# Loading and normalizing the first token block in two column halves, one warm-up matmul fewer, and later logit sums, in a fused attention and gated-MLP kernel

## The chip, the cores and the metric

One NeuronCore of one Trainium2 chip. The metric is device time of one execution in microseconds (us); "span" is the shorter time that the profile shows between first and last instruction. In these kernels the time is the span plus 1.7 to 1.8 us.

Engine names in profile lines: PE is TensorE's matmuls, PEld its weight loads, DVE VectorE, ACT ScalarE, POOL GpSimd, SP SyncE. "SPq" is an instruction that the sync engine's sequencer spends on issuing a DMA.

## The reference

```python
xn = layernorm(x)                                  # x: 2048 tokens x 512, bf16
# A: 32 heads of 16, each query looks at 8 keys, 2 apart, behind it
qkv    = xn @ wqkv
logits = einsum('bhsd,bhswd->bhsw', q, gathered_k) * scale     # + mask
o      = einsum('bhsw,bhswd->bhsd', softmax(logits), gathered_v) @ wo
# B: MLP with a spatial gate
z  = gelu(xn @ w_in)                               # 2048 x 1792
z1 = z[:, :896];  z2 = layernorm(z[:, 896:])
g  = einsum('ts,bsf->btf', w_sp, z2) + b_sp        # w_sp: 2048 x 2048
return x + o + (z1 * g) @ w_out
```

## The kernel before

A planner gets tasks (`T(engine, function, reads, writes, est, name)`), orders them on each engine by estimates, and sets the semaphores. The order on an engine is fixed when the kernel is built; each engine then runs its tasks in that order. PE's tasks for this argument, in order: ten warm-up matmuls, the first block's transposes, the z2 stage (`z2`, with the right half of `w_in`), the projections Q and K, ..., the z1 stage, the logit sums scattered among these, then the spatial gate.

The loads at the start. x blocks are 128 tokens (128 KB). The z2 weights come in two column halves, "a" and "b", each split over the sync and the scalar queue:

```python
ld_x(0, "sp")                       # block 0, sync queue
ld_x(1, "act")                      # block 1, scalar queue
ld_win_h("w_in2a", FH, HF)          # first half of the z2 weights, on both queues
ld_x(2, "sp"); ld_x(3, "act")
ld_win_h("w_in2b", FH + HF, HF)     # second half, on both queues
...
```

The first block: statistics and aggregate on DVE, power on POOL, normalization on DVE, four transposes on PE, two evictions.

```python
def ln_block(b):
    T("dve", bn_stats(Fv("st6", 6, 9 * b), xin), reads=[("xin", xs_)] + ..., name="bnst%d" % b)
    T("dve", bn_aggr(...), name="bnag%d" % b)
    T("pool", tensor_tensor(rstd, mv, mhalf, ALU.pow), name="rstd%d" % b)
    T("dve", tensor_scalar(xn, xin, mean, rstd, subtract, mult), name="norm%d" % b)
    ...
    T("pe", tr, reads=[("xn", sl), "ident"], name="xTr%d" % b)      # four 128x128 transposes
    ...
```

The logit sums. VectorE multiplies queries by shifted keys into one of four product buffers `pb`; PE sums two buffers at a time with 16 matmuls. `margin` is how much later than a product's estimated end the planner puts its sum:

```python
T("dve", lambda v: v.tensor_tensor(pbv, qb, kb, ALU.mult), reads=rd, writes=[("pb", s_)], name="prod%d_%d" % (j, c), ...)
...
T("pe", mm, reads=[("pb", (s_ - 1) % NPB), ("pb", s_), "E8"], writes=["psl"],
  est=4 * 232.0 + 100, name="red%d_%d" % (j, c), margin=cfg.get("m_red", 800.0))
```

The last sum, `red3_3`, reads buffers 2 and 3. Behind it comes the spatial gate. It needs `w_sp` transposed, in four pieces of 2 MB (`wT0` to `wT3`) that take turns in two places. The second place lies on memory that the logit stage used:

```python
lay(base, ("Sn", 3 * NK * 384), ("wT1", WSL), ...)                # wT1: elements 9216 to 17408 from base
lay(base, ("QT", 4096), ("KT", 8 * (512 + KP)), ("pb", NPB * 4096))  # pb: buffer 2 begins at 16512
```

So `wT1` covers product buffers 0, 1 and the first 896 elements of buffer 2, and its load has to wait for the last logit sum. The first consumer of `wT1` on PE is a slice of four matmuls (`gp6_1_0`, line 1053 before, 1078 after), which stands between the fourth and the fifth of the seven products of the gate's first quarter. The products of each quarter also need differences within that quarter's `wT`, which VectorE makes: four instructions of 1.22 us per quarter, `T1`, `T2`, `T4` and `T3` with the quarter's number (line 960 before, 985 after). `T3_3`, of the last quarter, is the last of them.

## Time and profile before

| before | |
|---|---|
| time | 237.72 us, median of 3 (237.45 to 238.06) |
| span | 236.0 us |
| PE busy | 230.8 us (98%) |
| first z2 matmul / second weights' half used / first projection | 6.71 / 7.81 / 14.03 us |
| last logit sums / their wait for the product | 100.72 / 0.86 us |

The page's busy line, PE's waits, the first 7 us and the hole at 100 us are shown in the prediction. The timeline of PE around the gate's first products (start us, us, engine, line, operation, count): the products begin at 111.20 and run into the slice that uses `wT1` (line 1053) at 115.02. The first row hides a wait of 0.149 us for ScalarE, before the product at 113.26; the view breaks a row only from 0.15 us on.

```profile
111.20 3.98 PE L1098 MATMUL ps<-arena 128*128 128x256 bf16 x32
115.02 1.03 PE L1053 MATMUL ps<-arena 128*128 128x512 bf16 x4
```

```profile
199.47 2.35 DVE L960 TENSOR_TENSOR arena<-arena 128x2048 bf16<-128x2048 bf16 x2
```

```profile
201.99 1.25 PE L1098 MATMUL ps<-arena 128*128 128x256 bf16 x10
```

VectorE stands idle for 0.93 us for a power on POOL, starts again at 90.89, and in that trace has no idle time above 0.11 us until `T3_3` ends at 201.82 (199.47 plus 2.35). The product that needs it starts 0.17 us later. So PE and VectorE come to this meeting point at nearly the same time, and after it PE alone sets the 34.2 us to the end.

### The profile page before, as it was taken

The numbers are of one execution on the slowest core, as the hardware profiler recorded it, in microseconds if no ns is written. First come the engines' busy times: TensorE is split into PE (matmuls) and PEld (weight loads), VectorE is DVE, ScalarE is ACT, GpSimd is POOL, SyncE is SP. The second block draws the span as 40 slices with busy tenths as digits, with TensorE's granted clock in tenths as the row PEclk, the third lists the DMA queues.
The fourth block names the chain that finished last, engine by engine and source line by source line (L and its number), as shares of the span: only waits on it lengthen the run. The fifth ranks groups of instructions, "written<-read, shape, count | busy, mean of one in ns | idle before, by whom it ended". The sixth has DMA issues, their size and how long they took to land.

```text
span 236.0 us, 3886 instructions
## 1 busy us (share of the span) xinstructions
PE 230.8 (98%) x1511; PEld 138.0 (58%) x1511; DVE 203.4 (86%) x231; ACT 143.7 (61%) x303; POOL 44.1 (19%) x74
## 2 busy tenths in 40 slices
PE   7999999999999999999999999999999999999996
PEld 3444444444444444345787777776777677777753
DVE  4688789989989898999999999999999999998022
ACT  2698678958889996659543554453445444554512
POOL 4555846477054013000000000000000000000000
PEclk9999999999999999999999999999999999999999
DMA  6987999802009900059504697484993664122302
GB/s 202 355 215 204 258 316 304 115 0 78 13 0 209 238 0 0 0 128 269 185 0 93 236 288 209 159 238 110 280 332 88 224 131 183 44 60 56 87 25 89
DMA packets 61698, 35.53 MB, mean 151 GB/s; under 512 B 49388, under 2 KB 60012, under 8 KB 60656
## 3 DMA queue, kind: packets, MB, share of 16 engines
q1 hardware_dynamic: 55040, 27.96, 45.9%
q10 hardware_dynamic: 5824, 5.21, 6.9%
q0 software_dynamic: 816, 2.12, 3.5%
q8 instruction: 12, 0.20, 0.3%
q14 instruction: 6, 0.05, 0.1%
HBM read 19.01 MB, written 4.21 MB: 98 GB/s over the span
## 4 chain that ended last, share of the span: by engine, by line
PE 82%; issue 6%; ACT 5%; DVE 4%; POOLq 1%; POOL 1%; ACTq 0%
PE ps L1098 31%; PE ps L1200 16%; PE ps L733 11%; PE ps L861 8%; PE ps L1053 4%; PE ps L713 4%; PE ps L878 3%; PE ps L772 3%; PE ps L636 2%; DVE arena L759 2%; DVE arena L937 1%; POOLq L399 1%; ACT L809 1%; POOL vscr L720 1%; ACT arena L809 1%
## 5 line engine op out<-in xcount | busy, mean ns | idle before, releaser
L1098 PE MATMUL ps<-arena 128*128 128x256 bf16 x672 | 79.0, 273 | 0.2
L1098 PEld LDWEIGHTS ps<-arena 128*128 128x128 bf16 x672 | 65.5, 98 | 15.0 <-ACT ps L1026 0.7
L1026 ACT ACTIVATE arena<-ps 128x256 bf16<-128x256 f32 (+2 forms) x43 | 20.1, 468 | 39.9 <-PE ps L1098 21.2
L1200 PE MATMUL ps<-arena 128*128 128x512 bf16 (+2 forms) x187 | 41.9, 366 | 0.0
L1147 DVE TENSOR_TENSOR arena<-arena 128x4096 bf16<-128x4096 bf16 x16 | 36.6, 2290 | 0.8
L759 DVE TENSOR_TENSOR arena<-arena 128x4096 bf16<-128x4096 bf16 x16 | 36.1, 2284 | 0.0
L1156 DVE TENSOR_TENSOR arena<-arena 128x4096 bf16<-128x4096 bf16 (+2 forms) x24 | 33.6, 1399 | 0.9
L733 PE MATMUL ps<-arena 128*128 128x512 bf16 x128 | 28.8, 379 | 0.0
L1200 PEld LDWEIGHTS ps<-arena 128*128 128x128 bf16 x187 | 19.6, 108 | 13.8
L861 PE MATMUL ps<-arena 128*128 128x448 bf16 x128 | 26.1, 353 | 0.4 <-DVE arena L696 0.2
L878 PE MATMUL ps<-arena 128*128 128x512 bf16 x112 | 24.9, 379 | 0.2 <-ACT arena L883 0.2
L733 PEld LDWEIGHTS ps<-arena 128*128 128x128 bf16 x128 | 12.3, 98 | 15.5 <-issue 1.3
L741 ACT ACTIVATE arena<-ps 128x1024 bf16<-128x1024 f32 x16 | 16.3, 1019 | 7.0 <-PE ps L733 6.3
L1026 ACT ACTIVATE ps<-ps 128x256 f32<-128x256 f32 x36 | 13.2, 366 | 11.8 <-PE ps L1098 10.8
L960 DVE TENSOR_TENSOR arena<-arena 128x2048 bf16<-128x2048 bf16 x16 | 19.4, 1220 | 0.8 <-DMA arena<-in_B_w_sp_dram 0.4
L883 ACT ACTIVATE arena<-ps 128x512 bf16<-128x512 f32 x28 | 15.7, 605 | 6.7 <-PE ps L878 6.5
L866 ACT ACTIVATE arena<-ps 128x448 bf16<-128x448 f32 x32 | 17.2, 545 | 4.1 <-PE ps L861 1.9
L861 PEld LDWEIGHTS ps<-arena 128*128 128x128 bf16 x128 | 11.9, 98 | 13.2 <-ACT arena L866 1.3
L1026 ACT ACTIVATE ps<-arena 128x512 f32<-128x512 bf16 (+3 forms) x33 | 16.7, 509 | 4.5 <-ACT arena L1026 3.0
L878 PEld LDWEIGHTS ps<-arena 128*128 128x128 bf16 x112 | 10.7, 98 | 14.0 <-ACT arena L883 1.1
L1053 PE MATMUL ps<-arena 128*128 128x512 bf16 x64 | 15.6, 379 | 0.0
L888 ACT ACTIVATE arena<-arena 128x896 bf16<-128x896 bf16 x16 | 15.1, 946 | 0.2
(67 smaller groups left out, 217.3 us busy)
## 6 DMA issues: line engine op xcount, KB each, us to landing
arena<-vscr SPq DMA_DIRECT2D x8, 1152.0 KB, 6.0
arena<-in_A_x_dram ACTq DMA_DIRECT2D x18, 128.0 KB, 2.6
vscr<-arena POOLq DMA_DIRECT2D x16, 128.0 KB, 5.2
arena<-in_A_x_dram SPq DMA_DIRECT2D x14, 128.0 KB, 6.7
out_dram<-arena ACTq DMA_DIRECT2D x14, 128.0 KB, 1.8
arena<-in_A_wqkv_dram SPq DMA_DIRECT2D x2, 512.0 KB, 7.8
arena<-in_B_w_in_dram SPq DMA_DIRECT2D x1, 896.0 KB, 5.2
arena<-in_B_w_out_dram SPq DMA_DIRECT2D x1, 896.0 KB, 6.2
```

The source lines that it names most:

```text
L733: last = t.matmul(bank(k + which), AC(off["wqk"] + 1024 * dc + col0, [[1, 128]]), AC(off["xnT"] + dc * S + 512 * j, [[1, 512]]), start=(dc ...
L759: T("dve", lambda v: v.tensor_tensor(pbv, qb, kb, ALU.mult), reads=rd, writes=[("pb", s_)], est=c_dve(4096, 2.0), name="prod%d_%d" % (j, c ...
L861: last = t.matmul(ps[:, 512 * k: 512 * k + HF], AC(off["xnT"] + dc * S + 128 * b, [[1, 128]]), AC(off["w_in2"] + FH * dc + c0, [[1, HF]]), ...
L866: T("act", (lambda k, hf: lambda a: a.activation(A("z2", HF, FH * b + HF * hf), ps[:, 512 * k: 512 * k + HF], ACTF.Gelu_apprx_tanh, accum_ ...
L878: lastm = t.matmul(bank(k), AC(off["w_in1"] + FH * dc + 128 * fc, [[1, 128]]), AC(off["xnT"] + dc * S + 512 * j, [[1, 512]]), start=(dc == ...
L960: T("dve", (lambda o_, x_, y_: lambda v: v.tensor_tensor(o_, x_, y_, ALU.subtract))(o_, x_, y_), reads=rd, writes=[wr], est=c_dve(NK * 256 ...
L1026: T("act", lambda a: a.activation(out_, in_, ACTF.Copy), reads=reads, writes=writes, est=c_act(n), name=name)
L1053: last = t.matmul(bank(k), AC(off["z2"] + FH * sh + 128 * fc, [[1, 128]]), AC(WT[r_] + sh * 512, [[1, 512]]), start=False, stop=(sh == NB ...
L1098: last = t.matmul(half(bk), lh(k), rh(k), start=False, stop=(k == NK - 1), skip_group_check=True)
L1147: T("dve", (lambda tv, iv, av: lambda v: v.tensor_tensor(tv, iv, av, ALU.mult))(tv, iv, av), reads=[("attn", j)] + ([("Ve", par)] if q < 2 ...
L1156: T("dve", (lambda o_, n: lambda v: v.tensor_tensor(o_, two(0, n), two(n, n), ALU.add))(o_, n), reads=[] if n > 512 else ["Vs", ("Ve", par ...
L1200: last = t.matmul(po, lh, rh, start=False, stop=(q == len(order) - 1), skip_group_check=True)
```

## The change

Its intent: reach the first useful matmul sooner, by loading the first block as two column halves on two queues and letting the statistics, the normalization and the transposes work half by half; and close PE's hole before the last logit sums by letting the planner put them later. The core of the diff:

```diff
-    warm=10,
+    warm=9,
...
-        ld_x(0, "sp")
-        ld_x(1, "act")
+        for h in range(2):
+            dma(("sp", "act")[h], ... A("xin", 256, 256 * h), x2[0:128, 256 * h: 256 * h + 256] ...)
+        ld_x(1, "sp")
         ld_win_h("w_in2a", FH, HF)
...
+        def ln_first():
+            for h in range(2):
+                T("dve", bn_stats(st0[6 * h], xin half h), name="bnst0%s" % "ab"[h])
+            T("dve", bn_aggr(mv, Fv("st0", 15)), name="bnag0")
+            T("pool", ... pow ..., name="rstd0")
+            for h in range(2):
+                T("dve", tensor_scalar(xn half h, xin half h, ...), name="norm0%s" % "ab"[h])
+                T("pe", tr, ...two transposes..., name="xTr0%s" % "ab"[h])
+            ... the two evictions and the two fill matmuls as before
...
-                  est=4 * 232.0 + 100, name="red%d_%d" % (j, c), margin=cfg.get("m_red", 800.0))
+                  est=4 * 232.0 + 100, name="red%d_%d" % (j, c), margin=cfg.get("m_red", 1600.0))
```

Cut: the memory and the two memsets of the statistics (DVE has four instructions more), and the general path with its first-block cases taken out. One more load on the sync queue: block 1 moved there, so the weights' sync halves are each one issue later.

## The prediction

> **What bounds the kernel now.** I read the page's busy shares first, then who PE waited for, then the order of time in the first 14 us and around 85 to 116 us. The busy share says that PE is the engine to look at:
>
> ```profile
> PE 230.8 (98%) x1511; PEld 138.0 (58%) x1511; DVE 203.4 (86%) x231; ACT 143.7 (61%) x303; POOL 44.1 (19%) x74
> ```
>
> Those 98% also hold warm-up matmuls that compute nothing, and ends that are modelled, so I checked spacing. In the long runs 32 matmuls of 512 columns take 6.91 us (0.216 us each) and 16 of 256 columns take 1.75 us (0.109 us each). At that spacing PE runs nearly without a hole from 14 us to 231 us. So the time is: the start until PE's first useful matmul, plus PE's work, plus the few holes in it, plus a tail (last matmul ends near 233.7, span 236.0). The holes are short:
>
> ```profile
> PE ps L636 <- DVE fpool L545: 1.3, 1, 1.3
> PE ps L772 <- DVE arena L759: 0.9, 1, 0.9
> PE ps L861 <- DVE arena L696: 0.2, 1, 0.2
> PE ps L878 <- ACT arena L883: 0.2, 1, 0.2
> ```
>
> The columns are us in total, times, longest. The first is the wait for the zeros before the warm-up. The second is one wait of the logit sums (L772) for the last product (L759). The third is the end of the first block's preparation, the fourth a filled set of PSUM banks.
>
> The start, in order of time, from the chain's window and the timeline (start, us, what):
>
> ```profile
> 3.35 0.69 DVE L664 BATCH_NORM_STATS2 fpool<-arena 128x6 f32<-128x512 bf16 x1 [1.94 <-DMA arena<-in_A_x_dram]
> 4.07 0.20 DVE L667 BATCH_NORM_AGGREGATE fpool<-fpool 128x2 f32<-128x9 f32 x1
> 4.36 0.58 POOL L669 TENSOR_TENSOR fpool<-fpool 128x1 f32<-128x1 f32 x1 [1.59 <-DVE fpool L667]
> 4.97 0.41 DVE L671 TENSOR_SCALAR arena<-arena,fpool 128x512 bf16<-128x512 bf16 x1
> 5.44 0.42 PEld L686 LDWEIGHTS ps<-arena 128*128 128x128 bf16 x4 [0.64 <-DVE arena L671]
> 5.50 0.54 PE L686 MATMUL ps<-arena 128*128 128x128 bf16 x4
> 6.07 0.42 DVE L696 CAST arena<-ps 128x256 bf16<-128x256 f32 x1 [0.58 <-PE ps L686]
> 6.71 0.92 PE L861 MATMUL ps<-arena 128*128 128x448 bf16 x4 [0.25 <-DVE arena L696]
> ```
>
> It is one serial chain: load (issued at 0.80), statistics, aggregate, power on POOL, normalize, four transposes, two evictions in parallel, first z2 matmul at 6.71. The transposes' weights are loaded at 5.44, and their matmul starts at 5.50, when the tenth warm-up matmul ends (ten at 0.427 us from 1.26 give 5.5).
>
> The mid-kernel hole:
>
> ```profile
> 91.06 8.81 PE L878 MATMUL ps<-arena 128*128 128x512 bf16 x40
> 100.72 1.05 PE L772 MATMUL ps<-arena 128*32 128x512 bf16 x16 [0.86 <-DVE arena L759]
> 101.70 6.22 PE L878 MATMUL ps<-arena 128*128 128x512 bf16 x28
> ```
>
> PE does 40 z1 matmuls, then stands for the product, then does the logit sums, then 28 more z1 matmuls that could have gone first. VectorE ends that product at about 100.67 (96.18 plus 4.49).
>
> **What the Trainium skill says.** "TensorE: Matmul & The Clock Gate", What's actually happening: the array starts at half clock and is released after a busy window of about 3.4 us, whose phase is free-running. The trace agrees in kind: warm-up matmuls come 0.43 us apart, later ones 0.216. The same page's "Wait — 56ns, not 53.3ns?" gives 426.7 and 215.7 ns for 512 columns, as seen here. "DMA: Bandwidth & Descriptors", Issuing engines are not separate DMA queues: two issuers save issue time, not movement. The two first loads here, issued at 0.80 and 0.81 on two queues, indeed share the engines. "VectorE: DVE Perf Modes", TRN2 errata: each instruction pays a fixed extra, so halving the elements does not halve the time. This trace shows it: aggregation of 9 numbers takes 0.20 us and statistics of 512 take 0.69.
>
> **The change part by part.**
>
> 1. Load in halves. The first block's 128 KB is no longer one load beside the second block's 128 KB, but two of 64 KB, first on each queue; block 1 moves to second on the sync queue. So the engines move 128 KB instead of 256 KB before the first block is complete. At the page's 355 GB/s of the second slice the 128 KB less is 0.36 us at most; with 512-byte rows I take 0.25: statistics can start near 3.10 instead of 3.35.
> 2. Statistics in halves. 0.69 us for 512 elements, with about 0.16 us fixed (512 at 0.96 per ns would be 0.53; an estimate), gives 0.42 for 256; the second, back to back, saves 0.04 as the second 512-element one does (0.65). Together about 0.80 against 0.69: a loss of 0.11. Aggregate over 15 numbers: still 0.20.
> 3. Normalize in halves: 0.41 becomes about 0.27 twice, the second overlapped by some 0.03: 0.51, a loss of 0.10. But the first two transposes now lie beside the second half's normalization, and after it only two of four remain: two at 0.107 us cold, a gain of 0.21. Net gain 0.11.
> 4. One warm-up matmul fewer: PE is free at 5.07 instead of 5.50. By itself it gains the 0.06 us between the weights (5.44) and the matmul (5.50); otherwise it only removes a block that the earlier chain would now meet. Warm and ready by chain: norm ends near 5.3, last transposes near 5.6, evictions (0.42) end near 6.3, z2 starts near 6.5 instead of 6.71.
> Sum of the start: 0.25 - 0.11 + 0.11 + 0.06, about 0.3; I take 0.2, since the chain has semaphore hops that I can't halve.
>
> Does it survive to 14 us? The z2 stage is a relay between PE and ScalarE (gelu eviction, then the next block's transpose eviction, then PE again at 8.84 and 10.99), so an earlier first z2 moves the later ones. One absolute edge is the second half of the weights, used at 7.80 in the kernel before. Its sync half now has a block more ahead of it. I count half of the 0.2 as at risk there.
>
> 5. Logit sums later. The planner's margin before a sum goes from 800 to 1600 ns. PE's alternative work comes in z1 groups of four matmuls, 4 x 0.216 = 0.86 us, so 0.8 us more margin is about one group more in front of the sums. In the hole at 100.72, one group put forward fills 0.86 us of about 0.93 (the matmul before starts at 99.48 and lasts 0.216; the sums start at 100.72; an ordinary entry to the sums costs 0.09). I take 0.8. No matmul is added, nothing on VectorE is removed. The other seven sums do not wait visibly, so their delay costs nothing, provided that their four product buffers are not wanted: the products trail the sums of two pairs earlier by over 3 us.
>
> Does it survive to the end? After the hole the softmax runs on VectorE at 104.17, behind two other additions, so it doesn't wait for sums ending one group later. The exponential sits on ScalarE at 109.06 to 112.26, and PE waits about 0.3 us for the seeds behind it at 113.26; both ScalarE's work before it (z1 evictions) and PE move together. From there to 231 us PE has no hole, and VectorE has slack (7.1 us of one wait on ScalarE), so a PE gain reaches the tail.
>
> Sum: 0.2 + 0.8 = 1.0 us off 237.72, so 236.7.
>
> **The rivals.**
>
> A. The gain at the start is eaten by the weights. For: w_in2 is used as soon as it is there at 7.80, and part 1 reorders the queues. Against: total bytes in front of it are the same. Then only the hole counts: 236.9.
> B. The order shift doesn't help: VectorE becomes the bound between 82 and 113 us. For: it is busy 26.97 of 28.30 us from 85 to 113.3, and its products follow power on POOL and a transposed weight load. If softmax is pushed behind another 2.3 us product, the exponential lands among the seeds, and PE pays there. Then 237.3 to 238.3. Against: the page shows VectorE with its own idle waits downstream.
> C. PE goes cold or warms up later because of one warm-up matmul fewer. For: the array reaches full speed only around 5.7 us here. If it came one window later, some 3.4 us of work would run at half clock: 1.7 us lost, 238.5. Against: there are transposes and two fill matmuls right after; the pause would be near 0.1 to 0.2 us.
> D. Both parts are worth more than counted, with the waits at 85.66 (0.2) and 113.26 (0.3) also filled by the new order: 236.0.
>
> **Range and chances.** Centre 236.7; A and B give the upper side, D the lower; C is a tail. Range 235.8 to 237.8. Two per cent is 4.75 us, more than the sum of all visible holes, so faster by over 2% has 1%; slower by over 2% would need a planner order that starves PE repeatedly, 2%; within, 97%.
>
> **What would show it.** Right: first statistics near 3.1 us in two pieces; first z2 matmul near 6.5; the PE wait on L759 gone or under 0.2 us; the same number of matmuls less one; PE busy near 230; the last matmul about 1 us earlier. Wrong: the wait for L759 still 0.9 us or come back under another name (ScalarE seeds, weights at 7.8); first z2 matmul at 6.7 or later; half-clock spacing after 6 us; a new VectorE wait between 36 and 113 us.

## More of the kernel before

A table by stretch: the stretch, its length, each engine's busy us with its number of instructions, the granted clock, the DMA share, and last the GB/s that the DMA engines moved.

```profile
2.00:4.00 2.00, 2.00 (x6) 0.76 (x5) 0.65 (x1) 0.72 (x1) 0.77 (x2) 1.00 0.98 294
...
91.00:202.00 111.00, 109.97 (x788) 76.03 (x785) 108.79 (x95) 57.49 (x124) 0.00 (x0) 1.00 0.62 168
```

In the second line, from 91 to 202 us, VectorE (the third pair) is busy for 108.79 of 111.00 us. The rest is some 0.02 us between each two of its 95 instructions. PE is busy for 109.97. And VectorE's and PE's timelines where that stretch begins and ends:

```profile
90.89 1.78 DVE L910 TENSOR_SCALAR arena<-arena,fpool 128x896 bf16<-128x896 bf16 x4 [0.93 <-POOL fpool L907]
```

## The result, and the profile after

The changed kernel took 238.27 us in the median of six runs (237.58 to 238.66); the kernel before, in the same rounds, 237.78 (237.45 to 241.07; the 241.07 is a slow run, and the median of the five others is 237.72). Executions over 1.5% slower than the fastest of the same kernel are left out of the means. A ratio in this document is the mean time of one kernel's runs over the mean of the other's runs of the same rounds, so not quite the ratio of the medians. Here it is 1.0019, with a 95% interval of 0.9997 to 1.0040: within 2%, and by its sign rather a loss, though the interval still holds 1. The prediction of 236.7, with a range to 237.8, was too low.

The traced run of the changed kernel was one of the two fastest of its six (237.71 us, span 235.9), the trace of before a typical one (237.73, span 236.0). So these two traces show why nothing was gained; what some of the other runs lost in addition is read from further traces below.

PE's busy time on the page fell from 230.8 to 230.4 us, by the one warm-up matmul. Whom PE waited for (us in total, times, longest). The wait for the product (0.9 before) is gone. New are 0.5 at the slice that uses `wT1` and 0.4 for the weights:

```profile
PE ps L1078 <- DVE arena L1090: 0.5, 1, 0.5
...
PE ps L886 <- DMA arena<-in_B_w_in_dram: 0.4, 1, 0.4
```

**The start.** VectorE's timeline of the changed kernel; the brackets tell how long it had stood idle and what ended that:

```profile
2.80 0.75 DVE L669 BATCH_NORM_STATS2 fpool<-arena 128x6 f32<-128x256 bf16 x2 [1.24 <-DMA arena<-in_A_x_dram]
4.40 0.69 DVE L703 BATCH_NORM_STATS2 fpool<-arena 128x6 f32<-128x512 bf16 x1 [0.59 <-DMA arena<-in_A_x_dram]
5.01 0.59 DVE L677 TENSOR_SCALAR arena<-arena,fpool 128x256 bf16<-128x256 bf16 x2
```

The halves land early: the statistics start at 2.80, not 3.35. But in VectorE's order block 1's statistics (line 703) stand ahead of block 0's normalization (line 677), and block 1 is now the second load of a queue. VectorE stands 0.59 us for it, and the normalization begins at 5.01, where it began at 4.97 before, although POOL's power was ready at 4.48 (3.90 plus 0.58). PE's timeline follows:

```profile
5.40 0.54 PE L684 MATMUL ps<-arena 128*128 128x128 bf16 x4 [0.41 <-DVE arena L677]
6.67 0.92 PE L886 MATMUL ps<-arena 128*128 128x448 bf16 x4 [0.29 <-DVE arena L692]
8.20 1.69 PE L886 MATMUL ps<-arena 128*128 128x448 bf16 x8 [0.39 <-DMA arena<-in_B_w_in_dram]
```

The first z2 matmul comes at 6.67 (6.71 before), but the second half of the weights is there only for 8.20 (7.81 before). The chain of work up to 15 us says the same in another way: in the changed kernel, it begins with five issues in a row on the sync queue and goes on (start us, us, what) through the weights to PE:

```profile
2.70 5.44 DMA arena<-in_B_w_in_dram
...
8.20 1.69 PE ps L886 x8
```

The kernel before issued that same half at 2.23, since one load fewer stood before it. And from 2 to 4 us the engines moved less; compare 294 GB/s before:

```profile
2.00:4.00 2.00, 2.00 (x6) 0.76 (x5) 0.97 (x3) 0.74 (x1) 0.87 (x3) 1.00 0.82 229
```

65 GB/s less for 2 us is 130 KB, and 130 KB at the 340 GB/s of the slices after it is 0.38 us: an estimate, close to the 0.39 us by which the weights came later. That may be chance, though: a lower rate would hold back both halves of these weights, and they moved apart. The part on the scalar queue landed at 7.40 (7.76 before), the part on the sync queue at 8.15 (7.34 before), so the block that was moved to the sync queue probably has its share. The repeat of the changed kernel shows 237 GB/s there, the repeat of the kernel before 294 again. The Trainium skill, "DMA: Bandwidth & Descriptors", Specifications, puts the least transfer for full rate at 512 bytes; the new rows are exactly 512 bytes, and while they move the rate is lower. No run here isolates the row size from the changed queues.

The first projection then starts at 14.13 (14.03 before).

In one point this trace misleads. Six traces have the changed start as it is (after, s2, s3, u1, v1, x1), six the start of before (before, s1, r2, v2, v3, x0); they come from several chips. Their means, changed against before: first statistics 2.89 and 3.47; first z2 matmul 6.38 and 6.62; the weights' sync part 8.32 and 7.62, their scalar part 7.66 and 7.95; first projection 14.35 (13.94 to 14.76) and 14.08 (13.96 to 14.27). So the first z2 matmul does come earlier in the mean, by 0.24 us. The first trace hides it because block 1 landed as late as 4.38 there (3.80 to 4.09 in the five others). The late sync part then turns the gain into a loss of 0.26 us in the mean.

**The middle.** PE's timeline of the changed kernel:

```profile
100.76 1.05 PE L797 MATMUL ps<-arena 128*32 128x512 bf16 x16
...
110.38 1.91 PE L1123 MATMUL ps<-arena 128*128 128x256 bf16 x16
112.44 1.92 PE L1123 MATMUL ps<-arena 128*128 128x256 bf16 x16 [0.15 <-ACT ps L1051]
114.86 1.02 PE L1078 MATMUL ps<-arena 128*128 128x512 bf16 x4 [0.50 <-DVE arena L1090]
```

One z1 group more stands in front of the sums (24 z1 matmuls follow them, not 28), and the 0.86 us hole before them is filled. The first product starts at 110.38 instead of 111.20: 0.82 us ahead. Then it is given back at the slice, which starts at 114.86 instead of 115.02: of 0.82 us, 0.16 is left. (The 0.15 for ScalarE, which makes the product's starting values, is no part of it: the kernel before has the same wait of 0.149. The profile counts 0.50 at the slice because the modelled ends of matmuls overlap the next start. From start to start the slice came 0.77 us after the matmul in front of it, where the spacing is 0.109; that is the 0.66 us given back.)

The first reason lies in the sums' own start, 100.76 against 100.72. They did not move, because VectorE's products set them; only PE's other work moved ahead of them. `wT1` may be issued only when the sums end, so it was issued at 101.85 (101.81 before) and landed at 114.72 (114.35 before). In the kernel before, PE came to the slice at 115.02 and the data was there; in the changed kernel PE could have begun it at 114.20 (0.109 us after the matmul at 114.09) and stood. The profile names VectorE's line 1090 as the releaser of that wait, as it ended last; that this isn't the cause is shown by the experiments.

**The meeting at 202 us.** VectorE's and PE's timelines of the changed kernel:

```profile
199.44 2.35 DVE L985 TENSOR_TENSOR arena<-arena 128x2048 bf16<-128x2048 bf16 x2
```

```profile
201.94 1.25 PE L1123 MATMUL ps<-arena 128*128 128x256 bf16 x10
```

VectorE's idle 0.93 us before its instruction at 90.77 is there as before, and from it to `T3_3`'s end at 201.79 VectorE has no idle time above 0.11 us, as before. It is 0.03 us earlier than in the kernel before (201.82), and so the product starts 0.05 us earlier and the span is 0.06 shorter (235.94 against 236.00). This is the second reason, and the deeper one: nothing that PE gains between 91 and 202 us can pass this point, unless VectorE passes it earlier too. The filled hole took nothing off VectorE's chain. (That a gain of PE alone stops here is shown by s3 below.)

### The profile page after: what moved, and what is told of

Its sections match the earlier page's. It is cut to its first block, busy times and chain, and to the rows that moved or that the text cites. A ratio compares the mean times of both kernels' runs of the same rounds, so it can differ in the third digit from the quotient of the medians.

```text
span 235.9 us, 3887 instructions
## 1 busy us (share of the span) xinstructions
PE 230.4 (98%) x1510; PEld 137.6 (58%) x1510; DVE 204.0 (86%) x235; ACT 143.7 (61%) x303; POOL 44.7 (19%) x74
## 4 chain that ended last, share of the span: by engine, by line
PE 76%; DVE 10%; issue 6%; DMA 2%; ACT 2%; POOLq 1%; POOL 1%; SPq 1%; ACTq 0%
PE ps L1123 30%; PE ps L1225 16%; PE ps L758 11%; PE ps L886 8%; PE ps L1078 4%; PE ps L738 4%; DVE arena L962 3%; DMA arena<-in_B_w_in_dram 2%; PE ps L797 2%; DVE arena L1172 2%; DVE arena L784 2%; POOLq L399 1%; POOL vscr L745 1%; DVE arena L1181 1%; ACT arena L766 1%
## 5 line engine op out<-in xcount | busy, mean ns | idle before, releaser
L1051 ACT ACTIVATE ps<-ps 128x256 f32<-128x256 f32 x36 | 13.2, 366 | 12.9 <-PE ps L1123 11.8
L772 POOL COPY arena<-arena 128x16 bf16<-128x16 bf16 x12 | 14.1, 1177 | 7.8 <-DVE ps L813 2.9
```

The lines of the kernel that those rows point to most:

```text
L1051: T("act", lambda a: a.activation(out_, in_, ACTF.Copy), reads=reads, writes=writes, est=c_act(n), name=name)
```

## The experiments

Theory T, to be tested: the start gain is lost because the weights' second half lands later and VectorE stands for block 1; the gain of the moved sums is lost because `wT1` is issued only after the sums. (`wT1` is the first reason above; the meeting at 202 us is not in these expectations.) The rivals: the warm-up matmul that was taken away (called W where an expectation uses a letter), VectorE's own work as the bound of the middle, and a loss that only the run-to-run scatter shows. The kernels of one batch ran on one chip together with the kernel before; batches are not compared with each other. Times are medians of six runs unless said otherwise; ratios are against the kernel before of the same batch.

| run | time us (range) | ratio (95%) |
|---|---|---|
| r1_warm10 | 238.25 (237.91 to 239.01) | 0.9979 (0.9945 to 1.0013) |
| r2_sums_moved | 238.62 (238.35 to 240.56) | 1.0006 (0.9967 to 1.0046) |
| r3_x1_halves | 238.92 (238.41 to 241.52) | 1.0021 (0.9976 to 1.0066) |
| r4_norm_first | 238.74 (238.25 to 238.94) | 0.9996 (0.9959 to 1.0032) |
| s1_before_again (one run) | 238.62 | |
| s2_after_again | 238.47 (237.94 to 241.14) | 1.0041 (1.0002 to 1.0080) |
| s3_w1_early | 238.10 (237.63 to 238.63) | 1.0010 (0.9986 to 1.0033) |
| s4_whole_load | 238.38 (238.00 to 239.33) | 1.0025 (0.9997 to 1.0054) |
| u1_w1_T3_early | 238.10 (237.96 to 238.62) | 1.0002 (0.9978 to 1.0026) |
| u2_queues | 237.80 (237.19 to 238.92) | 0.9980 (0.9951 to 1.0008) |
| u3_queues_norm | 238.09 (237.72 to 238.62) | 0.9998 (0.9974 to 1.0023) |
| u4_all | 237.63 (237.17 to 238.42) | 0.9982 (0.9956 to 1.0008) |
| v1_start_only | 238.95 (238.51 to 239.36) | 1.0009 (0.9988 to 1.0029) |
| v2_order_only | 238.03 (237.44 to 238.92) | 0.9972 (0.9950 to 0.9995) |
| v3_order_w1_T3 | 237.31 (237.14 to 237.41) | 0.9937 (0.9919 to 0.9955) |
| x0_fixed_again | 237.53 (237.38 to 238.15) | 0.9952 (0.9931 to 0.9973) |
| x1_fixed_halves | 237.88 (237.31 to 238.17) | 0.9959 (0.9937 to 0.9980) |
| x2_fixed_half_work | 237.33 (237.17 to 237.71) | 0.9941 (0.9922 to 0.9959) |

The kernel before, by batch: r 238.84, s 237.76, u 237.89, v 238.69, x 238.58, with ranges of 1.8 to 2.8 us. It scatters more than any effect in question, so the traces have to carry most of the argument. In the diffs, `move(engine, task, after)` shifts one task in one engine's fixed order.

### r1_warm10: the warm-up matmul put back

```diff
-    warm=9,
+    warm=10,
```

> The changed kernel with ten warm-up matmuls again, all else as changed. In the profiled run of the changed kernel the array was already at full spacing in the 9th warm-up matmul (4.6 us), yet four of its six runs were 0.4 to 1.0 us longer than that run. Theory W (the pause between the ninth warm-up matmul and the transposes sometimes delays the release of the clock): the slow runs vanish, the median falls to about 237.7, ratio to the kernel before 0.998 to 1.000. Rival J (the spread comes from transfers that now end a wait of PE, at 8.2 and 114.8 us): same median as the changed kernel, 238.0 to 238.4, ratio 1.001 to 1.003.

238.25 us. In its trace the weights' second half lands at 8.37 (8.15 in the first trace of the changed kernel), z2's second half starts at 8.51 and the first projection at 14.65, so the start is no better; span 236.5. The tenth matmul doesn't bring the gain back, and rival W has no support, but the interval (0.9945 to 1.0013) is too wide to give the matmul a size of its own.

### r2_sums_moved: the kernel before, with the last sum one z1 group later

```diff
+ move("pe", "red3_3", after="z1_0_3")
```

> The kernel before with one edit: the last logit sums stand behind one more z1 group of four matmuls on PE; no other order moves. Theory T (the load of the second transposed w_sp block is issued when these sums have ended, because it overwrites the product buffers that they read; it lands some 12 us later, and then bounds the next slice): PE's wait of 0.9 us at L772 goes to under 0.1, PE reaches the slice of L1053 after the four products 0.8 us earlier, waits there 0.3 to 0.7 us, and starts it near 114.8 instead of 115.0; total 0.0 to 0.2 us less, ratio 0.999 to 1.000. Rival S (what was predicted: the filled hole is kept to the end): the slice starts near 114.2 and the total falls by 0.8, ratio 0.9965.

238.62 us, no faster. In this trace `wT0` landed late (83.15), so VectorE stood 0.8 us for it and the products were late: the sums started at 101.69, `wT1` landed at 116.04, and the slice waited 1.0 us and began at 116.39. The wait that the moved sum removed came back at the slice, though here with a late `wT0` on top, which the edit didn't ask for. VectorE carried that lateness on: `T3_3` ended at 202.77, and the span was 237.3.

### r3_x1_halves: block 1 as two row halves on both queues

```diff
- block 1 (128 rows) on the sync queue
+ rows 0 to 63 on the sync queue, rows 64 to 127 on the scalar queue
```

> The changed kernel with the second token block's load cut into two row halves, one second on each queue, so that both queues again carry the same bytes ahead of the weights' second half. Theory Q (the uneven queues made that half land at 8.14 instead of 7.76, and the second block at 4.37 instead of 3.49, which held the in-order VectorE in front of the first block's normalization): second block lands near 3.6, normalization starts near 4.5 instead of 5.01, first z2 matmul near 6.2, the wait on the weights shrinks, the second z2 half starts near 7.8 instead of 8.20, the first matmul of L758 near 13.7 instead of 14.13. Whether the total follows: if PE is free to keep it, 0.4 less than the changed kernel; if VectorE and the w_sp load bound 85 to 115 us (theory T), 0.1 or less.

238.92 us. It failed in its purpose: the normalization started at 5.31, later than the changed kernel's 5.01, the weights landed at 8.65 and the projection started at 14.86. With one more issue ahead of them, the two parts of the weights were issued at 2.98 and 3.26 (2.26 and 2.70 in the changed kernel); in this one trace that cost more than the shared load brought.

### r4_norm_first: block 1's statistics behind block 0's normalization

```diff
+ move("dve", "bnst1", after="norm0b")
```

> The changed kernel with one edit of VectorE's order: the second block's statistics stand behind the first block's two normalizations instead of ahead of them. Theory Q: normalization starts near 4.55 instead of 5.01 and the first z2 matmul near 6.2 instead of 6.66, but the second z2 half still waits for the weights until 8.2, so that the first matmul of L758 stays at 13.9 to 14.2 and the total is that of the changed kernel within 0.2. Rival: the stall of VectorE is what cost the start; then L758 starts near 13.7 and the total falls by 0.4.

238.74 us. VectorE's and PE's timelines of this kernel:

```profile
4.48 0.60 DVE L677 TENSOR_SCALAR arena<-arena,fpool 128x256 bf16<-128x256 bf16 x2 [0.70 <-POOL fpool L673]
```

```profile
6.48 0.92 PE L886 MATMUL ps<-arena 128*128 128x448 bf16 x4 [0.62 <-DVE arena L692]
...
8.63 1.10 PE L886 MATMUL ps<-arena 128*128 128x448 bf16 x5 [1.01 <-DMA arena<-in_B_w_in_dram]
```

The stall of VectorE is removed: the normalization starts at 4.48, the moment POOL is done, and the first z2 matmul at 6.48, as the prediction had it. But the edit isn't what brings that. In s2, the changed kernel once more, block 1 landed at 4.01, its statistics stood in front as ever, and the first z2 matmul came sooner still:

```profile
6.30 0.92 PE L886 MATMUL ps<-arena 128*128 128x448 bf16 x4 [0.29 <-DVE arena L692]
```

In r4 the moved statistics stand in front of VectorE's eviction (line 692) instead, and PE waits 0.62 us for that. Either way the earlier matmul is worth nothing: PE then stands 1.01 us (0.80 in s2) for the weights' second half, until 8.63 (8.24). So the start is set by that load, not by the chain of the first block.

### s1_before_again, s2_after_again: both kernels once more, unchanged

> The kernel before, unchanged, for a second trace on the same chip as the next three. Every theory: as before, with the first matmul of L733 near 14.0 to 14.2, PE's wait of 0.9 us at L772 near 100.7, the slice of L1053 after the products at about 115.0. What is to be learned is how far landings of transfers move from chip to chip: the first transposed w_sp block landed 11.2 us after its issue in the first trace.

> The changed kernel, unchanged, for a second trace and more rounds. Theory Q (uneven queues and half-row transfers delay the weights' second half): that half lands at 8.1 to 8.7, the second z2 half starts at 8.2 to 8.7, the first matmul of L758 at 14.1 to 14.8, 0.1 to 0.7 later than in the kernel before on this chip; total within 0.3% of it.

The changed kernel: 238.47 us, ratio 1.0041 (1.0002 to 1.0080). One run of 241.14 us at a clock of 0.993 is in that mean; without it the ratio is 1.002, so this is no sure loss. Its trace (span 236.6) repeats the first one: weights at 8.19, projection at 14.18, slice at 115.16. Here VectorE's line 1090 ended only at 115.34, after the slice had begun, so it can't have released it, and the page names the load:

```profile
PE ps L1078 <- DMA arena<-in_B_w_sp_dram: 0.5, 1, 0.5
```

The kernel before: 238.62 us in a single run, span 236.9. Its projection starts at 14.03 as in the first trace, but its first logit sum already at 37.4 instead of 36.4, and PE's waits for products sum to 1.7 us in two waits. So the kernel before has a slower form of its own, nearly 1 us longer, and comparisons of single runs say nothing.

### s3_w1_early: `wT1` moved off the buffers that the last sum reads

```diff
-    ... ("KT", 8 * (512 + KP)), ("pb", NPB * 4096))
+    ... ("KT", 8 * (512 + KP)), ("pad", FH), ("pb", NPB * 4096))   # scrap of the z2 norm goes to pad
```

The 896 elements before `pb` shift it so that `wT1` covers only buffers 0 and 1. All orders are pinned to those of the changed kernel.

> The changed kernel with every engine's order as it is, but a layout in which the second transposed w_sp block overwrites only the first two product buffers (the scrap output of the squares fills the gap), so that its load waits for the sums near 91 us, not for those near 100.8. Theory T: the load is issued near 92.1 instead of 101.9 and lands before 106; the slice of L1078 after the products starts when they end, near 114.2 instead of 114.86, and the total falls by 0.5 to 0.7 against the changed kernel. Rival (the wait at 114.86 is for VectorE's update of L1090, as the profile names it): start and total as in the changed kernel.

238.10 us (1.0010; the changed kernel in the same batch 1.0041, with overlapping intervals). The load is issued at 91.9 and lands at 101.49. PE's timeline at the slice, then at 202 us, and VectorE's there:

```profile
113.95 1.03 PE L1080 MATMUL ps<-arena 128*128 128x512 bf16 x4
```

```profile
201.68 1.92 PE L1125 MATMUL ps<-arena 128*128 128x256 bf16 x16 [0.55 <-DVE arena L987]
```

```profile
199.27 2.35 DVE L987 TENSOR_TENSOR arena<-arena 128x2048 bf16<-128x2048 bf16 x2
```

The slice comes at 113.95, with no wait, 0.91 us earlier than in the changed kernel: the 0.5 us wait was for `wT1`, not for line 1090. The rest of the theory's gain isn't there: the span is 235.9 as in the first trace of the changed kernel, because PE now stands 0.55 us for VectorE at 202 us.

The list of waits says "line 987, 0.5" without a time, and I took it for `T3_0`, which ends near 114.3, close to the slice. Asked by stretch of time, the wait lies between 200 and 220 us, and it is for `T3_3`. The repair of `T3_0` in the runs below rests on that misreading.

### s4_whole_load: the changed kernel with the loads of before

```diff
- two column halves of block 0 first on both queues, block 1 second on sync
+ block 0 whole on sync, block 1 whole on scalar; statistics and normalization stay in halves
```

> The changed kernel with the first block loaded whole on the sync queue and the second whole on the scalar queue, as before the change; statistics, normalization, transposes stay in halves, and all engines' orders stay. Theory Q: statistics start near 3.35, the second block lands near 3.5, normalization of the first half starts near 4.9 to 5.0; the weights' second half lands near 7.8 and the second z2 half starts at 7.8 to 7.9; the first matmul of L758 near 13.9 to 14.1, 0.3 to 0.6 earlier than the changed kernel on this chip, and the total follows by as much, since the later stages are a chain that starts from there. Rival: the delay comes from the changed order of work on PE and ScalarE; then the second z2 half stays at 8.2 or later.

238.38 us, against the expectation. In its trace block 3's load landed late (7.39), the weights at 8.67, the projection started at 14.73. One trace with a late transfer; undecided here, and taken up again as x2. The chain of this kernel at 100 us shows the edge in the middle plainly: sums, then the load, then the slice.

```profile
101.42 0.98 PE ps L797 x16
...
102.45 12.92 DMA arena<-in_B_w_sp_dram
115.36 0.14 issue
115.50 1.02 PE ps L1078 x4
```

### u1_w1_T3_early: s3, with `T3_0` earlier on VectorE

```diff
+ move("dve", "T3_0", after="pv2")       # on top of s3_w1_early
```

> The layout of s3_w1_early (second w_sp load issued after the sums near 91 us) and, on VectorE, the in-place difference T3 (the second product block's operand) put ahead of the first addition of the value sums instead of behind it. In s3 the slice began 0.9 us earlier but the next product then waited 0.5 us for that difference. Theory T: with both out of the way no wait over 0.2 us is left on PE between the sums near 100.7 and 125 us; the slice starts near 113.9 to 114.2, the product after it 0.86 later, and the total is 0.8 to 1.0 below the changed kernel on this chip, ratio to the kernel before 0.996 to 0.999. Rival: another edge stands within 0.3 us of these two; then only 0.2 more than s3 is gained.

238.10 us (1.0002). The same wait is back: PE stands 0.51 us at 202.20 for line 987, so the move of `T3_0` was beside the point. The traced run also started late (weights at 8.44, projection at 14.64).

### u2_queues, u3_queues_norm: the queues evened out

```diff
- block 2 on sync, block 3 on scalar, as in the changed kernel
+ block 2 on scalar, block 3 on sync behind the weights' second half     # u2
+ move("dve", "bnst1", after="norm0b")                                   # u3 adds this
```

> The changed kernel with the third block's load moved to the scalar queue and the fourth's to the sync queue behind the weights' second half, so that both queues carry 640 KB up to the end of that half. Theory Q: the two parts of that half land within 0.3 us of each other instead of 0.7 apart, the later near 7.5 instead of 8.1 to 8.5; the wait for it falls from 0.4 to 0.8 us to under 0.1, the second z2 half starts near 7.5, the first matmul of L758 near 13.5 to 13.8; the total falls by at most 0.4, since the second w_sp load and VectorE still bound 85 to 115 us. Rival: landings there are only scatter; then no change.

> u2_queues with the second block's statistics behind the first block's normalization on VectorE, as in r4_norm_first. There the first z2 matmul started 0.2 us earlier and then waited for the weights. Theory Q: with the weights there, the first z2 matmul starts near 6.2 and the second half at 7.4 to 7.6 (the weights), the first matmul of L758 near 13.4 to 13.6, at most 0.2 better than u2; total as u2 within 0.2.

237.80 and 238.09 us, ratios 0.9980 and 0.9998, both undecided. The traced runs were among the slower of each. Against the idea, the weights' later half landed at 9.21 (u2) and 8.32 (u3), and the projections started at 15.41 and 14.75. In u2 PE stood 1.88 us for the weights. Counting loads per queue doesn't foresee when a shared set of engines finishes one of them. Why u2's were that late stays open.

### u4_all: all repairs together, on the changed start

```diff
+ s3's layout, T3_0 after pv2, bnst1 after norm0b, u2's queues
+ move("dve", "prod3_2", after="prod3_1")
```

> All of the above together, and one product of VectorE (the third of the last wave) put between the power on POOL and the four normalizations that wait 0.93 us for it. Theory: start 0.5 earlier, the sums of the last wave without a wait at about 100.1, no wait over 0.2 us from there to 125; last matmul 1.3 to 1.6 earlier than the changed kernel on this chip; ratio to the kernel before 0.993 to 0.997. If VectorE is still the bound, the sums of the last wave wait and the total is that of u1.

237.63 us, 0.9982 (0.9956 to 1.0008): best of its batch by the median, not settled. Its trace (238.42, the slowest of six) has the projection at 14.90, the sums at 101.97 and the slice at 115.63. VectorE's idle time at 91 us is gone, since `prod3_2` now stands there, but 0.53 us of it comes back at 111.8; the late start (14.90) would account for the rest.

### v1_start_only and v2_order_only: the change taken apart

```diff
# v1: the changed kernel; every task that both kernels have stands in the order of before
# v2: the kernel before; orders pinned to those of the changed kernel
```

> The changed kernel's first-block work (halved loads, statistics, normalization, transposes, nine warm-up matmuls), with every engine's order otherwise pinned to that of the kernel before. Theory: statistics start near 2.8 to 2.9, but the second block lands near 4.0 and the weights' second half near 8.2, so the second z2 half starts at 8.0 to 8.5 and the first matmul of L758 at 14.0 to 14.6; PE's wait of 0.9 us at the last sums is back; total equal to the kernel before or up to 0.6 longer, ratio 1.000 to 1.003. What was predicted for this part alone: 0.2 less, ratio 0.999.

> The kernel before with every engine's order pinned to that of the changed kernel behind the first block; its start is that of before. Theory T: no wait at the last sums, PE at the first product 0.8 us earlier relative to them, then a wait of 0.4 to 0.9 us for the second w_sp load at the slice of L1053; total 0.0 to 0.2 less, ratio 0.999 to 1.000. What was predicted for this part alone: 0.8 less, ratio 0.9965.

With the changed start alone: 238.95 us, 1.0009 (0.9988 to 1.0029). PE's waits are the weights' and, back again, the product's:

```profile
PE ps L888 <- DMA arena<-in_B_w_in_dram: 1.2, 1, 1.2
PE ps L799 <- DVE arena L786: 0.9, 1, 0.9
```

With the changed order alone: 238.03 us, 0.9972 (0.9950 to 0.9995), a small gain whose interval just leaves out 1. The first product starts at 110.33, as in the changed kernel, and the slice waits as there (line 1055 is the slice here):

```profile
115.02 1.02 PE L1055 MATMUL ps<-arena 128*128 128x512 bf16 x4 [0.63 <-DVE arena L1067]
```

`wT1` landed at 114.88. In this pair of traces the order brings nothing at the slice (115.02 in both), so the measured 0.7 us between the medians is more than theory T foresaw. A part of it can be seen: the changed order also issues `wT0` at 69.7 instead of 70.8, and VectorE's wait for it fell from 0.4 us before to 0.2 here (0.7 in v1, which has the old order, 0.8 in r2). That makes the kernel less exposed to a late transfer. The interval also allows 0.1 us. The changed order is also more than one moved sum: set side by side, the two lists show that the larger margin moved all eight sums on PE and, with them, more than a dozen tasks on VectorE and a few on the other engines. Only r2 moves the last sum alone.

### v3_order_w1_T3: the order, with the load's edge moved and VectorE's hole filled

```diff
+ # on v2: s3's layout
+ move("dve", "T3_0", after="pv2")
+ move("dve", "prod3_2", after="prod3_1")
```

> v2_order_only, with the layout that lets the second w_sp load be issued at 92 us, VectorE's T3 ahead of the first addition, and the third product of the last wave put where VectorE waits for POOL. Theory T: no wait over 0.2 us on PE from the sums to 125 us; total 0.8 to 1.0 below v2, ratio to the kernel before 0.995 to 0.998. Rival: a fourth edge (the seeds behind the exponential, or VectorE) takes it; ratio 0.999.

237.31 us (237.14 to 237.41), 0.9937 (0.9919 to 0.9955): faster than the kernel before in the same rounds by 0.6%, and with a range of 0.3 us. Its timelines, PE's at the slice, VectorE's at 90 us and at 199 us, PE's at 201 us:

```profile
114.15 1.03 PE L1055 MATMUL ps<-arena 128*128 128x512 bf16 x4
```

```profile
87.93 4.49 DVE L761 TENSOR_TENSOR arena<-arena 128x4096 bf16<-128x4096 bf16 x2
92.34 1.77 DVE L912 TENSOR_SCALAR arena<-arena,fpool 128x896 bf16<-128x896 bf16 x4
```

```profile
198.88 2.35 DVE L962 TENSOR_TENSOR arena<-arena 128x2048 bf16<-128x2048 bf16 x2
```

```profile
201.38 1.91 PE L1100 MATMUL ps<-arena 128*128 128x256 bf16 x16
```

The slice comes 0.87 us earlier than in v2. On VectorE two products (line 761) stand together at 87.93 and run to 92.34: `prod3_2` fills the time in which VectorE stood 0.93 us for POOL, and the instruction after it has no wait in brackets any more. `T3_3` ends at 201.24 (201.97 in v2), the product that needs it starts at 201.38 (202.03), the span is 235.5 (236.2). Here both engines reach the meeting point earlier, so the time falls. I put `prod3_2` there for another reason; that it is the part which shortens VectorE's chain is read from the traces, and no run moves it alone. The 0.6% is against a kernel before that ran at 238.69 in this batch, about 1 us above its first runs; between the traced runs of v3 and before lie 0.47 us (237.26 and 237.73).

### x0, x1, x2: what the changed start costs when nothing hides it

All three have v3's repairs. x0 is v3 again, with the start of before. x1 has the whole changed start. x2 has the changed work in halves and nine warm-ups, but the loads of before.

```diff
# x1 against x0: + halved loads, + halved work, - one warm-up matmul
# x2 against x0:                 + halved work, - one warm-up matmul
```

> v3_order_w1_T3 once more, as the reference of this call. All theories: runs within 0.4 us of each other, ratio to the kernel before 0.992 to 0.997, first matmul of L735 near 14.0.

> As x0, but with the changed kernel's whole start. Theory Q (the half-row loads move fewer bytes per us and the sync queue carries a block more, so the weights' second half lands near 8.3 instead of 7.9): first matmul of the Q and K projections at 14.1 to 14.6, total 0.2 to 0.5 longer than x0. The prediction: 0.2 shorter.

> As x1, but the first block comes whole on the sync queue and the second whole on the scalar queue, as in the kernel before; statistics, normalization and transposes in halves, nine warm-up matmuls. Theory Q: weights land near 7.9, first matmul of the projections at 13.9 to 14.2, total within 0.15 of x0. Rival (the halved work or the missing warm-up matmul costs the time): total as x1.

| trace | weights' later half lands | projection starts | slice | `T3_3` ends | span | mean time of six |
|---|---|---|---|---|---|---|
| x0 | 8.21 | 14.27 | 114.35 | 201.43 | 235.72 | 237.62 |
| x1 | 8.77 | 14.76 | 114.76 | 201.92 | 236.19 | 237.83 |
| x2 | 8.28 | 14.26 | 114.33 | 201.43 | 235.72 | 237.38 |

Only x1, with the halved loads, is later at the start (PE stands 1.0 us for the weights), and its 0.49 us stays almost whole to the end (0.47 in the span).

In the means of six, x1 is 0.21 us over x0 and 0.45 over x2. The 0.45 is clear of the scatter of the runs, the 0.21 is not. x2 is no slower than x0, so no cost of halving the work and dropping a warm-up was found; the loads in halves, with block 1 behind them on the sync queue, cost some 0.2 to 0.5 us. x2 has the load edit of s4 and starts as x0 does, so s4's late start was most likely its own late transfer.

### All traces, read for the meeting at 202 us

| trace | projection starts | slice | `T3_3` ends | span | span less `T3_3` |
|---|---|---|---|---|---|
| before | 14.03 | 115.02 | 201.82 | 236.00 | 34.17 |
| s1, before again | 14.03 | 115.84 | 202.70 | 236.89 | 34.18 |
| after | 14.13 | 114.86 | 201.79 | 235.94 | 34.15 |
| s2, after again | 14.18 | 115.16 | 202.45 | 236.60 | 34.16 |
| s3 | 13.94 | 113.95 | 201.63 | 235.85 | 34.23 |
| v2 | 13.96 | 115.02 | 201.97 | 236.18 | 34.21 |
| v3 | 14.07 | 114.15 | 201.24 | 235.53 | 34.29 |

The slice moves over 1.9 us and doesn't foretell the span: s3 has the earliest slice, and v3, 0.2 us behind it there, ends 0.3 us before it. The end of VectorE's `T3_3` does: in all twenty traces the span is 34.15 to 34.38 us longer, but for r2 with 34.53, where PE was late by its wait of 1.0 us at the slice. And `T3_3` follows the start of VectorE's chain: in the fifteen traces without the moved `prod3_2` it ends 110.90 to 111.25 us after the wait for POOL. VectorE has no other wait in that stretch in before, after and s3, so it isn't PE that holds `T3_3` back. In the four runs with `prod3_2` moved and the other orders the same (v3, x0, x1, x2), `T3_3` ends 187.16 to 187.17 us after the first projection; in the fifteen it is 187.41 to 188.68 (before 187.79, after 187.66).

## Why the prediction was wrong

The class, within 2%, was right; the time was 1.6 us too low, and no part of the sum was kept. By its own steps:

1. *Load in halves, "statistics can start near 3.10 instead of 3.35".* Better than that: 2.80. (The 355 GB/s behind it is the rate from 5.9 to 11.8 us; at the 294 GB/s of 2 to 4 us the 128 KB are 0.45 us, so 0.36 was no upper limit.) Statistics in halves took 0.75 us for both (0.80 predicted), the normalization 0.59 (0.51 predicted). The costs of the work were right within 0.1 us.
2. *The sum of the start, a gain of 0.2, with the first z2 matmul near 6.5.* Missed in the first trace (6.67 against 6.71): the step looked at block 0's chain and not at VectorE's order, in which block 1, moved behind block 0 on the sync queue, stands in front of block 0's normalization. But in the means of six traces each the first z2 matmul is 0.24 us earlier (6.38 against 6.62), so the step's size was right. What fails is that the gain lasts, the next step.
3. *"Total bytes in front of it are the same", by which rival A was held to be at most a loss of the gain.* This is the failed step at the start. The bytes are the same, but the rate was not (229 against 294 GB/s from 2 to 4 us) and the sync half was issued at 2.70 instead of 2.23. The weights' later half was 0.39 us later in the first pair of traces (8.15 against 7.76) and 0.37 in the means of six. The prediction counted half of 0.2 us as at risk; the changed loads turned it into a loss, of 0.11 us at the first projection in that pair, of 0.26 in the means and of 0.49 in x1 against x0.
4. *One warm-up matmul fewer.* No effect found (r1, x2). Rival C, a clock that is released later, isn't supported: the traced start of both kernels shows full-speed spacing by the first z2 matmul. The moment varies from trace to trace, with nine as with ten: the spacing of 0.427 us for 512 columns has ended by 4.1 us in v1 and still holds at 5.5 us in u1 (both nine), it has ended by 4.6 us in v3 and still holds at 5.1 us in the kernel before (both ten).
5. *The sums later, "I take 0.8", and "from there to 231 us PE has no hole, and VectorE has slack ... so a PE gain reaches the tail".* The size at the hole was right: 0.86 us filled, 0.82 at the first product. That it reaches the tail is the failed step, and it failed twice. First, it didn't ask what may be *issued* only when the sums have ended: `wT1`'s load of 12.5 to 12.9 us runs beside everything; before, it landed 0.68 us ahead of its use. In the changed kernel PE came 0.82 us earlier and the load landed 0.38 us later, and 0.16 us was left (s3 shows that the wait was the load's). Second, VectorE has no slack: it is busy 108.79 of 111.00 us from 91 to 202, and at 202 us PE was 0.1 us behind it at most. The 7.1 us of one wait on ScalarE that the step leaned on as slack lie after 202 us in the trace of before, where they help nothing.
6. *Rival B, VectorE as the bound, 237.3 to 238.3.* In kind this is the way it went, but not by the path that it named: nothing was pushed among the seeds, for which PE waits as long as before (0.15 us). It was looked for from 82 to 113 us only, and held unlikely for VectorE's waits "downstream", of which there are none up to 202 us. Its range holds the measured 238.27 partly by luck, since the start's loss is in that too.

By size, in the first pair of traces: the start lost 0.11 us to the first projection instead of gaining 0.2; from there VectorE's chain to `T3_3` was 0.14 shorter (among other shifts its 0.42 us wait for `wT0` is gone, since the changed order issues that load 1 us earlier, and a wait of 0.94 for POOL at 51 us; against that a new one of 0.75 for ScalarE stands at 62.5, one of the prediction's own signs of being wrong); the tail gave 0.03. Together 0.06 us of span instead of 1.0; the traced runs differ by 0.02 (237.71 against 237.73). The median of the changed kernel lies 0.56 us above its traced run. Starts of the changed loads scatter between 13.94 and 15.41 us for the first projection over the traces here (queue edits included), those of the loads of before between 13.96 and 14.27 with one at 14.73. That can hold the rest, but the slower runs of that round were not traced, and so it is not shown.

What stays open: what `prod3_2` alone, or with `wT1` alone, would bring; why evening out the queues made the later half land later still; whether the 512-byte rows or the one issue more cost the more; how much of v2's gain is the earlier `wT0`; and that v1 and v2 (1.0009 and 0.9972) make 0.998 together, where the whole change measured 1.0019 and 1.0041 on other chips; their intervals barely meet.

## What to carry to other kernels

Before counting a filled hole of the busiest engine as a gain, find the next point where that engine meets another's chain, read from the timeline how late each arrives, and take the smaller slack as the most that can be gained; a second engine without a hole up to that point is a bound even at 86% over the whole span. Count among the chains the transfers that the moved instruction itself releases, as a load into reused memory. Splitting a load so that its first consumer starts sooner can move other loads back, as here, and a wait in a list has to be given its time before it is given a cause.

## What the Trainium skill lacked or had wrong

- "DMA: Bandwidth & Descriptors", Issuing engines are not separate DMA queues: it says that several issuers save only issue time. That section has no number for an issue (the page's only one is a count of cycles for earlier chips, in its part on trn3). In the first 3 us of the traces of before and after each plain issue on the sync queue took 0.40 to 0.47 us, and one more in front put the weights' half from 2.23 to 2.70.
- "DMA: Bandwidth & Descriptors", Specifications: 512 bytes is given as enough for full rate. With 512-byte rows at the front of the queues the engines moved 229 to 265 GB/s from 2 to 4 us (the six traces named above), with 1024-byte rows 277 to 294. Not isolated from the queue change, so a hint only.
- "VectorE: DVE Perf Modes", TRN2 errata: it gives a fixed extra per instruction, but no time for an instruction of statistics nor for two halves back to back. Here two statistics of 256 took 0.75 us where one of 512 took 0.69, two normalizations of 256 0.59 where one of 512 took 0.41.
- No page that I read says that a load into reused memory has to be counted as released by the last reader of any byte of it. Here an overlap of 896 of 8192 elements beyond the buffers already free held a transposed load back by 9.9 us (issued at 101.85, without the overlap at 91.9), and its issue to landing took 12.9 us.
